# One weight tile of 128 partitions loaded in three pieces of 112, 15 - g and 1 + g partitions, in a decode attention kernel

## The chip, the cores and the metric

The kernel runs on one core of a Trainium2 chip. The metric is the device time of one execution in microseconds (us), taken as the median of several runs. Beside the runs stands one execution that the hardware profiler recorded; the views quoted in this text come from it.

## The reference

One token is decoded. Part A is attention of 32 heads with 65536 cached keys and values each, and an output projection; part B is a small gated feed-forward network; a sigmoid gate mixes the two.

```python
# x: 1x1x512, k_cache, v_cache: 1x32x65536x128 (bf16), wq: 512x4096, wo: 4096x512
q = (x @ wq) as 32 heads of 128
scores = einsum(q, k_cache) * 128 ** -0.5
p = softmax(scores)
o = einsum(p, v_cache)
a = o.reshape(1, 1, 4096) @ wo
b = (silu(x @ w_gate) * (x @ w_up)) @ w_down      # F = 1792
g = sigmoid((x * gate_w).sum())
out = g * a + (1 - g) * b
```

The caches hold 32 heads x 65536 x 128 x 2 bytes, twice: 1073.7 MB. All the weights together are 13.9 MB, of which `wo` is 4.2 MB.

## The kernel before

The caches are read in tiles of 4 MB: 128 partitions x 16384 elements of bf16. A head has G = 4 key tiles and 4 value tiles, so there are N = 128 of each. All of them go through `ring`, a pool of SLOTS = 5 buffers of that size, which `wq`, the gate and up weights and the down weights use as well at the start.

**Key tiles.** VectorE multiplies a key tile with the head's query (L220) and halves the 128 columns three times by adding (L224) down to 16; TensorE adds up the last 16 against an identity matrix (L234, `scores`). Once a head has all four tiles, its maximum, exponentials and sum are taken (`row_max`, `exponentials`, `total`).

**Value tiles.** TensorE multiplies the probabilities with the value tile, 32 matmuls of 128x512 per tile (L282, `values`). After a head's last value tile, `head_out` brings its output into one column of `oT` (L306 to L317), and `project` (L327) multiplies that column with the head's 128x512 part of `wo` and adds it into `a_ps`.

**Order.** The program fixes the order on every engine itself (`manual_schedule`). The list `steps` pairs a key tile with a value tile: values run G = 4 tiles behind keys at first and LAG = 8 later. In each step the loads are issued first, key tile, then (in one step of 16) the next group of `wo`, then the value tile. All loads are issued from SyncE's queue (SP), one after the other: a load that must wait for a free buffer holds up those behind it. The semaphores that tell of landings come from eight lanes used in turn, so a load also waits until the load eight places before it has landed.

**The last loads.** The value tiles of the last head come in halves, and the very last tile in four pieces of 64, 32, 16 and 16 columns (`CUTS`), so that the matmuls on the first pieces (`last_values`, L295) run while the last piece is on its way. Then come `weigh` (L317), `project` (L327), a cast (L398) and the store of the output (L399).

**wo.** `load_wo(g)` fetches group g of four heads (WG = 4) into a tile of 128 partitions x 4 x 512, out of `wo_pool` with two buffers. Partition p takes four rows of `wo`, one for each head, so each partition receives four runs of 1 KB. Group 0 is loaded at the start, behind the feed-forward weights; group g + 1 is loaded when value tile 16 g + 8 is due, and its first projection comes some 12 value tiles later. There are H / WG = 8 groups.

Of the kernel before, what the change touches and what calls it, by code (L numbers as in the profile page):

```python
# [11 lines left out]
P = 128  # L12
# [7 lines left out]

LAG = 8
SPREAD = 40

CUTS = (0, 64, 96, 112, 128)

# [2 lines left out]
def kernel(  # L28
# [14 lines left out]
    nc = tc.nc  # L43
# [99 lines left out]
    wo_tiles = {}  # L143

    def load_wo(g):
        wo_tiles[g] = wo_pool.tile([P, WG, D], bf16, name="wo_sb")
        rows = A_wo[g * WG * P : (g + 1) * WG * P, :]
        nc.sync.dma_start(out=wo_tiles[g], in_=rows.rearrange("(h p) n -> p h n", p=P))

    load_wo(0)  # L150

    def feed_forward_in():
# [185 lines left out]
    for n in range(N):  # L338
        due = n >= G and not (n >= SPREAD and n % 4 == 3 and n - v < LAG)
        steps.append((n, v if due else None))  # L340
# [6 lines left out]
    for n, v in steps:  # L347
        if n is not None and n > 1:
            load(K_tiles, A_k_cache, n, "K_t")
        if v is not None:  # L350
            if v % (WG * G) == 2 * G and v // (WG * G) + 1 < H // WG:
                load_wo(v // (WG * G) + 1)
            halves = (0, NB // 2, NB) if v >= N - G else (0, NB)
            load(V_tiles, A_v_cache, v, "V_t", CUTS if v == N - 1 else halves)
# [75 lines left out]
```

## Time and profile before

| | |
|---|---|
| Time, median of 3 runs | 2544.31 us (2544.15 to 2545.1) |
| The profiled execution's own time | 2544.7 us |
| Its span, first to last instruction | 2542.9 us |
| DMA: share of 16 engines' span on queue q1 | 99.6% |
| Moved | 1088.63 MB, mean 428 GB/s |
| VectorE busy | 2174.6 us (86%) |
| TensorE busy | 1721.1 us (68%) |
| ScalarE busy | 75.9 us (3%) |
| Mean granted TensorE clock | 0.752 |
| `wo` loads | 8 of 512 KB, median 36.6 us from issue to landing |

The span is what the profile covers; 1.8 us of the profiled execution's own time lie outside it. "Share of 16 engines" is the time that all packets of a queue took, divided by sixteen times the span: the core has 16 DMA engines, and a transfer is shared out among them. A transfer has landed when all of the engines that carried it have reported, and the trace keeps the time of each of these reports, without the number of the engine. Queue q1 carries the program's own transfers; q8 and q14 are marked as carrying instructions.

### The profile page before, as it was taken

To read this page: it belongs to the slowest core of one execution; us is meant where nothing else is said; L and a number is where in the kernel's file an instruction comes from. 1 tells how busy PE (TensorE), PEld (TensorE's weight loads), DVE (VectorE), ACT (ScalarE), POOL (GpSimd) and SP (SyncE) were. 2 spreads that over 40 slices of the span, in tenths; PEclk is the share of its full clock that TensorE was granted. 3 is DMA by queue.
4 is the path that set the end of the run, shared out by engine and by line. 5 is a ranking of instruction groups with operands and counts; after the bars stand their busy time and mean duration, and the time that the engine had idled before them with its cause. 6 is when DMAs were issued, how large, how long until landed. Compare 5 with 4: busy or idle time off the path is not lost.

```text
span 2542.9 us, 15396 instructions
## 1 busy us (share of the span) xinstructions
PE 1721.1 (68%) x6818; PEld 705.6 (28%) x6818; DVE 2174.6 (86%) x779; ACT 75.9 (3%) x206; POOL 0.7 (0%) x6
## 2 busy tenths in 40 slices
PE   3576766766677656667676676667666676677768
PEld 2232222222222222222232222222222222222223
DVE  6999888888888999998888888888888888888870
ACT  1000000000000000000000000000000000000000
POOL 0000000000000000000000000000000000000000
PEclk7677777777777677776777777777777777777779
DMA  9999999999999999999999999999999999999998
GB/s 408 427 432 430 432 430 432 431 429 431 431 432 430 429 432 431 431 432 431 429 431 431 432 429 430 432 430 431 429 432 432 430 432 428 433 431 431 432 431 348
DMA packets 42884, 1088.63 MB, mean 428 GB/s; under 512 B 4673, under 2 KB 8770, under 8 KB 9026
## 3 DMA queue, kind: packets, MB, share of 16 engines
q1 hardware_dynamic: 42818, 1087.66, 99.6%
q8 instruction: 53, 0.87, 0.1%
q14 instruction: 13, 0.11, 0.0%
HBM read 1087.64 MB, written 0.00 MB: 428 GB/s over the span
## 4 chain that ended last, share of the span: by engine, by line
DMA 68%; PE 21%; DVE 11%; issue 1%; ACT 0%; SPq 0%; DVEq 0%
DMA V_t<-in_A_v_cache_dram 63%; PE O_ps L282 19%; DVE K_t L220 6%; DVE K_t L224 5%; DMA K_t<-in_A_k_cache_dram 4%; PE S_ps L234 1%; DMA wq_t<-in_A_wq_dram 0%; PE qg_ps L120 0%; DVE m L246 0%; PE oh_ps L308 0%; PE a_ps L207 0%; ACT P_sb L259 0%; DVE top L255 0%; ACT O_sb L306 0%; PE a_ps L327 0%
## 5 line engine op out<-in xcount | busy, mean ns | idle before, releaser
L282 PE MATMUL O_ps<-V_t,P_sb 128*4 128x512 bf16 x4064 | 1139.3, 450 | 499.6 <-DMA V_t<-in_A_v_cache_dram 497.4
L220 DVE TENSOR_TENSOR K_t<-K_t,q_bc 128x16384 bf16<-128x16384 bf16 (+1 forms) x159 | 1117.2, 7026 | 275.3 <-DMA K_t<-in_A_k_cache_dram 256.0
L224 DVE TENSOR_TENSOR K_t<-K_t 128x2048 bf16<-128x2048 bf16 (+3 forms) x477 | 1030.6, 2161 | 14.2
L282 PEld LDWEIGHTS <-P_sb 128*4 128x4 bf16 x4064 | 389.4, 96 | 1229.9 <-issue 883.3
L234 PE MATMUL S_ps<-K_t,ident_b 128*128 128x128 bf16 x2048 | 464.6, 392 | 123.8 <-DVE K_t L224 123.8
L234 PEld LDWEIGHTS <-ident_b 128*128 128x128 bf16 x2048 | 225.6, 114 | 346.9 <-issue 153.1
L308 PE MATMUL oh_ps<-ident_f,O_sb 4*128 4x1 f32 x256 | 57.2, 340 | 74.0 <-ACT O_sb L306 74.0
L250 PE MATMUL mT_ps<-diag,ones_f 128*128 128x128 f32 x64 | 23.6, 468 | 80.8 <-ACT diag L248 80.8
L308 PEld LDWEIGHTS oh_ps<-ident_f,O_sb 4*128 4x128 f32 x256 | 54.5, 310 | 83.1 <-ACT O_sb L306 78.8
L248 ACT ACTIVATE diag<-ident_f,m 128x128 f32<-128x128 f32 x32 | 12.8, 401 | 2108.3 <-DVE m L246 2108.3
L398 DVE CAST out_sb<-a_ps 1x512 bf16<-1x512 f32 x1 | 0.7, 677 | 52.4 <-PE a_ps L327 52.4
L250 PEld LDWEIGHTS mT_ps<-diag,ones_f 128*128 128x128 f32 x64 | 14.8, 288 | 96.6 <-ACT diag L248 96.6
L246 DVE TENSOR_REDUCE m<-S_ps 128x1 f32<-128x512 f32 x32 | 21.9, 684 | 7.4 <-PE S_ps L234 7.4
L259 ACT ACTIVATE P_sb<-S_ps,bias 128x512 bf16<-128x512 f32 x32 | 22.0, 687 | 1.0
L306 ACT ACTIVATE O_sb<-O_ps 4x512 f32<-4x512 f32 x32 | 18.3, 573 | 123.1 <-PE O_ps L282 123.1
L120 PE MATMUL qg_ps<-wq_t,X_bc 128*128 128x512 bf16 x32 | 8.5, 431 | 14.1 <-DMA wq_t<-in_A_wq_dram 14.1
L185 PE MATMUL b_ps<-wd_t,hT 128*1 128x512 bf16 x14 | 5.7, 597 | 15.7 <-DVE hT L178 15.7
L273 DVE RECIPROCAL recip<-tot_ps 128x1 f32<-128x1 f32 x32 | 5.1, 160 | 12.2 <-PE tot_ps L268 12.2
L327 PE MATMUL a_ps<-wo_sb,oT 128*1 128x512 bf16 x32 | 13.5, 423 | 0.4 <-ACT oT L317 0.4
L268 PEld LDWEIGHTS tot_ps<-rowsum,ones_f 128*128 128x128 f32 x64 | 9.5, 188 | 14.0 <-issue 14.0
L268 PE MATMUL tot_ps<-rowsum,ones_f 128*128 128x1 f32 x64 | 12.2, 260 | 0.0
L317 ACT ACTIVATE oT<-oh_ps,rg 128x1 bf16<-128x1 f32 x32 | 8.4, 264 | 81.2 <-PE oh_ps L308 75.0
(39 smaller groups left out, 69.1 us busy)
## 6 DMA issues: line engine op xcount, KB each, us to landing
K_t<-in_A_k_cache_dram SPq DMA_DIRECT2D x128, 4096.0 KB, 35.3
V_t<-in_A_v_cache_dram SPq DMA_DIRECT2D x124, 4096.0 KB, 29.7
V_t<-in_A_v_cache_dram SPq DMA_DIRECT2D x7, 2048.0 KB, 31.8
wq_t<-in_A_wq_dram SPq DMA_DIRECT2D x1, 4096.0 KB, 12.4
wo_sb<-in_A_wo_dram SPq DMA_DIRECT2D x8, 512.0 KB, 36.6
gu_t<-in_B_w_gate_dram SPq DMA_DIRECT2D x1, 1792.0 KB, 34.7
gu_t<-in_B_w_up_dram SPq DMA_DIRECT2D x1, 1792.0 KB, 38.4
wd_t<-in_B_w_down_dram SPq DMA_DIRECT2D x1, 1792.0 KB, 42.2
```

What stands on the lines that cost most here:

```text
L220: yield nc.vector.tensor_tensor(out=K, in0=K, in1=q_rep, op=ALU.mult)
L224: yield nc.vector.tensor_tensor(out=K[:, :, 0:half], in0=K[:, :, 0:half], in1=K[:, :, half : 2 * half], op=ALU.add,)
L234: nc.tensor.matmul(S_tiles[h][:, g * NB : (g + 1) * NB], lhsT=ident_b, rhs=K_tiles[n][:, :, c], start=(c == 0), stop=(c == WIDTH - 1),)
L246: nc.vector.tensor_reduce(out=m, in_=S_tiles[h], axis=AXIS.X, op=ALU.max)
L248: nc.scalar.activation(out=diag, in_=ident_f, func=ACT.Copy, scale=m)
L250: nc.tensor.matmul(mT_ps, lhsT=ones_f, rhs=diag, start=True, stop=True)
L259: nc.scalar.activation(out=P_tiles[h], in_=S_tiles[h], func=ACT.Exp, bias=bias, scale=scale, accum_out=rowsum[:, h : h + 1],)
L268: nc.tensor.matmul(tot_ps, lhsT=ones_f, rhs=rowsum[:, h : h + 1], start=True, stop=True)
L282: nc.tensor.matmul(O_tiles[h], lhsT=P_tiles[h][:, g * NB + j : g * NB + j + 4], rhs=V_tiles[n][:, j : j + 4, :], start=(g == 0 and j == 0) ...
L306: nc.scalar.activation(out=O_sb, in_=O_tiles.pop(h), func=ACT.Copy)
L308: nc.tensor.matmul(oh_ps, lhsT=O_sb[:, c * Dh : (c + 1) * Dh], rhs=ident_f[0:4, c : c + 1], start=(alone and c == 0), stop=(alone and c == 3),
L327: nc.tensor.matmul(a_ps, lhsT=oT[:, h : h + 1], rhs=wo_tiles[h // WG][:, h % WG, :], start=False, stop=(h == H - 1),)
```

## The change

`load_wo` no longer issues one transfer for the 128 partitions of a group but three: partitions 0 to 111, the next 15 - g, and the last 1 + g. The bytes, the tile, its place in the order and everything that reads it stay as they are. Over the eight groups the second piece has 15, 14, ... 8 partitions and the third 1, 2, ... 8.

```diff
+WO_BULK = 7
...
     def load_wo(g):
         wo_tiles[g] = wo_pool.tile([P, WG, D], bf16, name="wo_sb")
         rows = A_wo[g * WG * P : (g + 1) * WG * P, :]
-        nc.sync.dma_start(out=wo_tiles[g], in_=rows.rearrange("(h p) n -> p h n", p=P))
+        rows = rows.rearrange("(h p) n -> p h n", p=P)
+        for a, b in ((0, 16 * WO_BULK), (16 * WO_BULK, P - 1 - g), (P - 1 - g, P)):
+            nc.sync.dma_start(out=wo_tiles[g][a:b], in_=rows[a:b])
```

The program's instructions on the compute engines are the same and in the same order; SP issues 16 more transfers. As each transfer takes the next of the eight semaphore lanes, the lanes that later loads wait on move as well. Behind each later group this asks for no landing that the ring of five buffers does not ask for anyway. At the start it does: the third piece of group 0 waits for the landing of `wq`, and the third key tile, which waited for `wq` and the queries made from it, now waits for the landing of the first key tile as well.

## The prediction

> **What bounds the kernel now.** I read the page's DMA rows first, then stretches of time, then the landing records, then SP's timeline.
>
> ```profile
> span 2542.9 us, 15396 instructions
> ...
> GB/s 408 427 432 430 432 430 432 431 429 431 431 432 430 429 432 431 431 432 431 429 431 431 432 429 430 432 430 431 429 432 432 430 432 428 433 431 431 432 431 348
> DMA packets 42884, 1088.63 MB, mean 428 GB/s; under 512 B 4673, under 2 KB 8770, under 8 KB 9026
> ...
> q1 hardware_dynamic: 42818, 1087.66, 99.6%
> q8 instruction: 53, 0.87, 0.1%
> q14 instruction: 13, 0.11, 0.0%
> ```
>
> The rate stays at 428 to 433 GB/s from the third slice to the last but one, and the packets fill 99.6% of sixteen engines' time. VectorE at 86% and TensorE at 68% have room. So the end is set by the DMA engines, and by the one with the most to do. The chain of waits runs through the value loads and the matmuls that free their buffers; with the engines full, that is the way the queue is refilled, not a second limit. The next view has us from:to, length, busy time of PE, PEld, DVE, ACT and POOL, the granted clock, the DMA share and GB/s.
>
> ```profile
> 1200.00:1210.00 10.00, 5.21 (x17) 1.77 (x17) 9.93 (x3) 0.00 (x0) 0.00 (x0) 0.59 1.01 427
> 2520.00:2526.00 6.00, 6.00 (x30) 2.38 (x28) 0.00 (x0) 0.00 (x0) 0.00 (x0) 1.00 0.98 411
> 2526.00:2528.00 2.00, 1.58 (x8) 0.51 (x6) 0.00 (x0) 0.00 (x0) 0.00 (x0) 1.00 0.70 293
> 2530.00:2532.00 2.00, 2.00 (x11) 0.69 (x9) 0.00 (x0) 0.00 (x0) 0.00 (x0) 1.00 0.54 227
> 2534.00:2536.00 2.00, 2.00 (x59) 1.98 (x55) 0.00 (x0) 0.00 (x0) 0.00 (x0) 1.00 0.47 186
> 2537.00:2538.00 1.00, 0.84 (x27) 0.69 (x24) 0.00 (x0) 0.00 (x0) 0.00 (x0) 0.50 0.06 25
> 2538.00:2540.00 2.00, 1.13 (x17) 0.58 (x17) 0.00 (x0) 0.27 (x1) 0.00 (x0) 0.50 0.00 0
> ```
>
> Here the engines run out one by one. A share of 0.54 is some nine of sixteen; 0.06 is a single one, alone on the last microsecond. The trace's landing records say how far apart they are. Each transfer has sixteen; those of the last one lie 0, 0.2, 0.3, 0.6, 0.7, 1.3, 3.3, 6.7, 9.2, 9.5, 10.2, 10.3, 10.6, 10.8, 11.0 and 12.4 us behind the first, 6.1 on average. So five engines are early, three in between, eight late, and one is last by 1.4 us. The last one's distance grows in steps of about 1.55 us: 3.1 us at 125 us, 6.2 at 878, 9.2 at 1639, 10.85 at 2019, 12.4 at 2477. The packets of q8 explain it: 53 of 16 KB, each some 1.05 us long, with lengths that recur after every eighth. Eight engines take turns to fetch them, and one such packet and the slower one beside it cost its engine about 1.55 us. At 115 us the queue ran dry for a moment (V tiles issued at 113.80 us); after that no engine but the early ones at the very end has an idle stretch. Whatever the last engine carries is paid for, microsecond for microsecond: from its last landing at 2538.5 us the tail of matmul, scale, projection, cast and store takes 4.4 us, whatever came before.
>
> **The change, part by part.**
>
> *Bytes moved between engines.* The eight `wo` transfers land 1.45 to 1.49 us after the transfer before them on the first engine (1.48 for group 0). That is eight partitions on each engine, 32 packets of 1 KB, thus 1.47 / 8 = 0.184 us a partition. How will the new pieces be shared out? The page's counts show both ends: 276 loads with 16 reports each make 4416, and 4673 - 256 (the 8-byte packets of `xT` and `gwT`) - 4416 leaves one report for the output store. A load of 128 partitions is spread evenly over 16; a transfer with one row went to one engine. 112 is 7 each; 15 - g and 1 + g have no even sixteenths. Bounds: an engine left out by both pieces in all groups loses 8 x 0.184 = 1.47 us; one that got all 16 partitions of the two pieces each time would gain 8 x (16 - 1) x 0.184 = 22.1 us over now. The nearest row is the even spread of the 276 loads, all of 128 partitions, so I take one partition per engine, with both pieces starting at the same end of the sixteen. Then the engine nearest that end carries 8 more partitions in all (+1.47 us), the next 7 more, the eighth 1 more; the ninth 1 less, the sixteenth 8 less (-1.47 us). Nothing else in the change can bring anything.
>
> [...]
>
> *16 more transfers.* The last tile's pieces are queued one behind another like these: the landings of its four pieces on the first engine are 2.49, 1.26 and 1.27 us apart for 1 MB, 512 KB and 512 KB, which is 8 packets of 0.312 or 0.157 us and 0.01 of rest. So a transfer within a full queue costs an engine about 0.01 us: 16 x 0.01 = 0.2 us at most. An exposed transfer would be 1.8 us (`xT`, `gwT`, issue to landing); the full queue is the cover, and without it 16 x 1.8 = 29 us would be due.
>
> *SP.* Each issue takes 0.43 us:
>
> ```profile
> 510.02 0.33 SPq L111 DMA_DIRECT2D V_t<-in_A_v_cache_dram  x1
> 513.58 0.33 SPq L111 DMA_DIRECT2D K_t<-in_A_k_cache_dram  x1
> 513.96 0.43 SPq L148 DMA_DIRECT2D wo_sb<-in_A_wo_dram  x1
> 529.98 0.33 SPq L111 DMA_DIRECT2D V_t<-in_A_v_cache_dram  x1
> ```
>
> Two more (0.9 us) fit into the 15.6 us in which SP waits for the next value tile's buffer. Even a late issue would be covered: a tile lands 30 to 35 us after its issue and takes 9.7 us of the engines, so about two more are queued ahead of it. Cost 0; uncovered, 8 x 0.9 = 7 us.
>
> *Waits at the start.* The third piece of group 0 waits for `wq` (14.05 us in SP's rows), and the third key tile, issued at 22.59 us, now waits for the first one, whose sixteen landings lie between 23.2 and 23.8 us. It goes up to 1.2 us later, while the queue holds work until group 0 lands at 47.3 us. The fourth and fifth key tiles (44.3 and 51.0 us) wait for landings that were over by 38. Cost 0. Until 115 us VectorE sets the pace (9.78 of 10 us busy at 100 to 110), so group 0's shift may be lost when the queue runs dry: seven groups then count, 1.29 instead of 1.47 us.
>
> *Readers of `wo`.* A projection waits for three landings instead of one, some 12 value tiles after the issue, over 200 us for a landing of 37. Cost 0.
>
> **The sum.** Last engine among the relieved eight: 0.2 to 1.5 us less; among the loaded eight: 0.2 to 1.5 more. The second-last is 1.4 us ahead, so it hardly cuts the gain. The records do not number the engines; the order in which they report at the start puts early and late ones side by side and decides nothing. I take the relieved side, as a choice, and the mean of one to eight partitions: 4.5 x 0.184 = 0.8 us. The profiled execution goes from 2542.9 + 1.8 = 2544.7 to 2543.9; it was 0.4 over the median, so the median goes from 2544.3 to 2543.5. 0.2% (5 us) is about what a measurement of this kernel can tell from no change.
>
> **The rivals.**
> - *Forecast, the last engine is relieved:* 2542.8 to 2544.1. For: the shift only reaches the end by the last engine, and half of the engines are relieved. 0.50.
> - *The last engine is loaded:* the eight fetching engines are those that get the second partition. 2544.5 to 2545.8, slower by less than 0.1%. 0.25.
> - *It cancels:* the last engine is near the middle, or the 0.2 us of completions eat the shift. 2544.1 to 2544.5. 0.18.
> - *An odd piece is not spread:* one engine takes all partitions of the small pieces, as one took the store's row. It gets up to 22.1 us more. If it is an early one it has 12.4 us to spare and ends 9.7 us late: 2554; if it is the last, 2566. It decides as soon as one engine gets over 67 partitions more (12.4 / 0.184). Against it: every load with many partitions is spread. 0.05, slower.
> - *More than the shift:* all of the imbalance gone is 12.4 - 6.1 = 6.3 us, 2538, just past 0.2%. Eight partitions can't do that. 0.02, faster.
>
> Runs scatter over 0.95 us, half of it on either side: low 2544.31 - 1.47 - 0.5 = 2542.3, high 2544.31 + 1.47 + 0.5 = 2546.3. That holds the first three cases, 0.93 less a little at the edges. Faster 0.02, same 0.93, slower 0.05.
>
> **What the profile after would show.** q1 with the same bytes, share at 99.6%, and the last landing at 2537.0 to 2538.3 instead of 2538.5 us: right. One engine alone for more than 1.4 us at the end: the loaded side. 1 KB packets piled on one engine, and a DMA share near 0.06 for ten microseconds: not spread. If slices in the middle fall below 428 GB/s, the small transfers cost what I put at 0.01 us. A landing spread that is the same with another time would prove the shift irrelevant.

## The result, and the profile after

The changed kernel takes 2569.13 us (median of 5 runs, 2566.54 to 2573.14), against 2544.15 us before (2543.03 to 2545.1) in the same comparison: a ratio of 1.01, interval 1.0089 to 1.011. It is 25 us slower, where 0.8 us less was forecast. The profiled execution took 2569.56 us, with a span of 2567.8 us.

The page's rows after, as shown of before:

```profile
span 2567.8 us, 15408 instructions
...
GB/s 404 428 431 412 431 431 432 432 408 432 431 432 431 409 431 432 431 430 425 412 431 432 430 415 420 431 430 432 405 426 431 431 432 399 433 431 430 432 432 350
DMA packets 43015, 1088.63 MB, mean 424 GB/s; under 512 B 4804, under 2 KB 8901, under 8 KB 9157
...
q1 hardware_dynamic: 42949, 1087.66, 99.7%
q8 instruction: 53, 0.87, 0.1%
q14 instruction: 13, 0.11, 0.0%
```

The bytes are the same and the engines are as busy as before (99.7%), but the same work took longer. The loss is not spread out: the rate stands at 428 to 433 GB/s in most slices and dips to 399 to 420 in a few, where a group of `wo` is loaded. What the engines do there is seen in stretches of 2 us around the third group, after first and then before (the last two columns are the DMA share and GB/s):

```profile
547.00:549.00 2.00, 2.00 (x11) 0.82 (x10) 1.97 (x2) 0.00 (x0) 0.00 (x0) 1.00 1.12 323
549.00:551.00 2.00, 2.00 (x11) 0.65 (x10) 0.42 (x1) 0.00 (x0) 0.00 (x0) 1.00 1.02 224
551.00:553.00 2.00, 2.00 (x11) 1.09 (x11) 0.00 (x0) 0.00 (x0) 0.00 (x0) 1.00 1.04 248
553.00:555.00 2.00, 1.60 (x8) 0.59 (x6) 1.01 (x1) 0.00 (x0) 0.00 (x0) 1.00 1.00 270
555.00:557.00 2.00, 0.00 (x0) 0.00 (x0) 2.00 (x1) 0.00 (x0) 0.00 (x0) 0.82 1.02 426
```

```profile
544.00:546.00 2.00, 2.00 (x11) 0.79 (x10) 1.97 (x2) 0.00 (x0) 0.00 (x0) 1.00 1.00 399
546.00:548.00 2.00, 2.00 (x11) 0.68 (x8) 0.78 (x1) 0.00 (x0) 0.00 (x0) 1.00 0.98 380
548.00:550.00 2.00, 2.00 (x10) 1.03 (x10) 0.49 (x1) 0.00 (x0) 0.00 (x0) 1.00 1.11 462
```

Before, the rate hardly falls while a group passes. After, it halves for about 8 us, and no engine is idle: the packets themselves are slow. In the trace the 1 KB packets of `wo` take 78 ns at the median instead of 46, and packets of 32 KB, which belong to the cache tiles beside them and were not touched by the change, take more than 1.4 us 593 times instead of 93, at worst 2.6 us (2.2 before) instead of the usual 1.215. Added up and divided by sixteen, the 1 KB packets cost 20.0 - 12.5 = 7.5 us more, and the excess of the 32 KB packets over 1.215 us rose from 7.8 to 26.3, by 18.5 us. The sum, 26 us, is the whole loss, and over two thirds of it fall on neighbours.

The other places that the prediction named:

```profile
512.71 0.33 SPq L113 DMA_DIRECT2D V_t<-in_A_v_cache_dram  x1
516.27 0.33 SPq L113 DMA_DIRECT2D K_t<-in_A_k_cache_dram  x1
516.64 1.25 SPq L152 DMA_DIRECT2D wo_sb<-in_A_wo_dram  x3
530.97 0.35 SPq L113 DMA_DIRECT2D V_t<-in_A_v_cache_dram  x1
```

SP issues the three transfers within 1.25 us and still waits 13 us for the next value tile's buffer. At the end of the span the engines run out one by one as before, 25 us later:

```profile
2552.00:2560.00 8.00, 5.46 (x81) 2.92 (x79) 0.00 (x0) 0.59 (x1) 0.00 (x0) 0.99 0.56 232
2560.00:2563.00 3.00, 3.00 (x56) 2.97 (x54) 0.00 (x0) 0.00 (x0) 0.00 (x0) 0.50 0.12 45
2563.00:2565.00 2.00, 1.45 (x28) 0.78 (x25) 0.07 (x1) 0.26 (x1) 0.00 (x0) 0.50 0.00 0
```

The last landing is at 2563.3 instead of 2538.5 us, and the sixteen landings of the last transfer are spread over 12.2 us instead of 12.4: the imbalance between the engines, at which the change could aim, is as it was.

### The profile page after: what moved, and what is told of

It is laid out like the page before. It is cut to its first block, busy times and chain, and to the rows that moved or that the text cites. A ratio compares the mean times of both kernels' runs of the same rounds, so it can differ in the third digit from the quotient of the medians.

```text
span 2567.8 us, 15408 instructions
## 1 busy us (share of the span) xinstructions
PE 1721.2 (67%) x6818; PEld 706.9 (28%) x6818; DVE 2174.6 (85%) x779; ACT 75.9 (3%) x206; POOL 0.7 (0%) x6
## 3 DMA queue, kind: packets, MB, share of 16 engines
q1 hardware_dynamic: 42949, 1087.66, 99.7%
## 4 chain that ended last, share of the span: by engine, by line
DMA 69%; PE 20%; DVE 9%; SPq 1%; issue 1%; ACT 0%; DVEq 0%
DMA V_t<-in_A_v_cache_dram 62%; PE O_ps L286 19%; DMA K_t<-in_A_k_cache_dram 7%; DVE K_t L224 5%; DVE K_t L228 4%; PE S_ps L238 1%; SPq L152 1%; DVE m L250 0%; PE oh_ps L312 0%; PE a_ps L211 0%; ACT P_sb L263 0%; DVE top L259 0%; SPq L113 0%; ACT O_sb L310 0%; PE a_ps L331 0%
## 5 line engine op out<-in xcount | busy, mean ns | idle before, releaser
L277 DVE RECIPROCAL recip<-tot_ps 128x1 f32<-128x1 f32 x32 | 5.1, 160 | 12.4 <-PE tot_ps L272 12.4
L272 PE MATMUL tot_ps<-rowsum,ones_f 128*128 128x1 f32 x64 | 12.2, 260 | 0.0
```

Source lines behind the costliest of these rows:

```text
L272: nc.tensor.matmul(tot_ps, lhsT=ones_f, rhs=rowsum[:, h : h + 1], start=True, stop=True)
```

## The experiments

The first question was what is slow: the number of transfers, the uneven pieces, or the place that the pieces have. Of `load_wo` only the transfers are shown. In all of them `rows` is the rearranged slice, as in the change. Each comparison has its own runs of the kernel before, so its time differs a little from one to the next.

**Three whole transfers.** As many as in the changed kernel, each of 128 partitions.

```diff
+        for a, b in ((0, 2), (2, 3), (3, 4)):
+            nc.sync.dma_start(out=wo_tiles[g][:, a:b], in_=rows[:, a:b])
```

> Each group of wo comes in three transfers, but of all 128 partitions: heads 0 and 1, head 2, head 3 (256, 128 and 128 KB). So there are as many transfers as in the changed kernel (24), and every engine carries in each what it carries in any 128-partition load. Theory P (placement: a DMA engine that writes other partitions than those it writes in a 128-partition load gets in the way of the engines that write there): 2544 us, within 2 of before. Theory N (number: each extra transfer costs some 1.6 us, 25 / 16): 2569. Theory U (uneven: the pieces that not all sixteen engines carry are at fault): 2544. In P and U the 1 KB packets take 46 ns at the median as before, in N they may take longer.

Measured: 2543.43 us against 2543.75, ratio 1.0 (0.9991 to 1.0009); 1 KB packets at 46 ns.

```profile
GB/s 408 428 434 429 430 431 432 431 428 431 431 431 431 430 430 431 432 431 431 429 432 430 431 429 431 432 430 432 429 431 432 432 430 429 432 431 430 433 430 354
```

There are no dips: 16 more transfers cost nothing that can be measured. The number is out.

**112 and 16 partitions.** Both pieces are even shares for sixteen engines.

```diff
+        for a, b in ((0, 112), (112, P)):
+            nc.sync.dma_start(out=wo_tiles[g][a:b], in_=rows[a:b])
```

> Two transfers per group, of 112 and 16 partitions, seven and one for each engine: no piece is uneven, but both are shifted against the places of a 128-partition load. P: most of the 25 us, 2560 to 2569, and 1 KB packets near 78 ns at the median as in the changed kernel. N: 8 extra transfers, 12.5 us, 2556.5. U: 2544.

Measured: 2568.2 us against 2543.75, ratio 1.01 (1.0085 to 1.0115), 1 KB packets at 78 ns, and the same half rate around the third group:

```profile
547.00:549.00 2.00, 2.00 (x11) 0.77 (x9) 1.11 (x1) 0.00 (x0) 0.00 (x0) 1.00 1.01 229
549.00:551.00 2.00, 2.00 (x10) 0.86 (x9) 0.00 (x0) 0.00 (x0) 0.00 (x0) 1.00 1.09 239
551.00:553.00 2.00, 2.00 (x11) 1.03 (x9) 0.00 (x0) 0.00 (x0) 0.00 (x0) 1.00 1.07 269
```

This has all of the change's cost without an uneven piece. What the uneven pieces do to the balance of the engines is lost in the scatter of these runs.

**64 and 64 partitions.**

```diff
+        for a, b in ((0, 64), (64, P)):
+            nc.sync.dma_start(out=wo_tiles[g][a:b], in_=rows[a:b])
```

> Two transfers per group, of partitions 0 to 63 and 64 to 127, four partitions for each engine. P: 2556 to 2575, since four partitions per engine are again not the places of a 128-partition load. [...] N: 2556.5. U: 2544.

Measured: 2574.93 us against 2543.75, ratio 1.0124 (1.0109 to 1.0139). That is 31 us, more than for 112 and 16, and at the upper end of what placement (theory P) led one to expect. Neither the number (12.5 us) nor unevenness (none) gives it.

**The whole transfer, and the uneven pieces beside it.** The pieces go into a spare tile that nothing reads.

```diff
+        nc.sync.dma_start(out=wo_tiles[g], in_=rows)
+        spare = spare_pool.tile([P, WG, D], bf16, name="spare")
+        for a, b in ((112, P - 1 - g), (P - 1 - g, P)):
+            nc.sync.dma_start(out=spare[a:b], in_=rows[a:b])
```

> Each group of wo comes in one transfer of 128 partitions as before, and the two small pieces of the changed kernel (15 - g and 1 + g partitions) come again, into a spare tile that nothing reads. So the uneven pieces and the number of transfers are those of the changed kernel, with the transfer of 112 made whole. Bytes: 0.5 MB more, 1.2 us. P: 16 instead of 128 shifted partitions a group, an eighth of 25, so 2546 to 2550. N: 2570. U: 2565 to 2571.

Measured: 2549.8 us against 2543.75, ratio 1.0023 (1.0014 to 1.0033). The uneven pieces are worth 6 us, of which an estimated 1.2 us are the extra bytes that only this run moves. If the parts add up, the other 19 to 20 us of the change come from the transfer of 112.

So the partitions that a transfer covers matter. The second question was whether that is a matter of the shape, of the reading side, or of the partitions that are written. Three runs keep the whole transfer and add 256 KB more per group to the spare tile, differently placed.

**Extra 256 KB, all partitions.**

```diff
+        nc.sync.dma_start(out=wo_tiles[g], in_=rows)
+        spare = spare_pool.tile([P, WG, D], bf16, name="spare")
+        nc.sync.dma_start(out=spare[:, 0:2], in_=rows[:, 0:2])
```

> Each group of wo comes in one transfer as before; heads 0 and 1 of it (256 KB, 128 partitions) come once more into a spare tile that nothing reads. This prices the bytes alone: half of 1.47 us a group, 5.9 us in all, 2549.6 us, in every theory. 1 KB packets at 46 ns.

Measured: 2549.55 us against 2543.96, ratio 1.0022 (1.0013 to 1.0031). The bytes alone cost 5.6 us; the 1 KB packets took 48 ns at the median, near the expected 46.

**Extra 256 KB to partitions 32 to 95.**

```diff
-        nc.sync.dma_start(out=spare[:, 0:2], in_=rows[:, 0:2])
+        nc.sync.dma_start(out=spare[32:96], in_=rows[32:96])
```

> As the run with the half columns, but the extra 256 KB are partitions 32 to 95 of the group, written to partitions 32 to 95 of the spare tile, four for each engine. [...] Theory S (shape: every transfer of fewer than 128 partitions disturbs, wherever it goes): half of the 31 us that 64 + 64 partitions cost, and the bytes, 2565 us.

Measured: 2549.37 us against 2543.96, ratio 1.0022 (1.0012 to 1.0032). Beside the 5.6 us of the bytes this placement costs nothing that can be measured; the 1 KB packets took 48 ns here too.

**Extra 256 KB, the same rows, to partitions 0 to 63.**

```diff
-        nc.sync.dma_start(out=spare[32:96], in_=rows[32:96])
+        nc.sync.dma_start(out=spare[0:64], in_=rows[32:96])
```

> The same 256 KB, read from the same rows as in the run before, with the same share for each engine, but written to partitions 0 to 63 of the spare tile. Only the destination differs. [...] Theory S: 2565 us, the same as the run before. Theory R (the reading side is at fault, the order of the rows in HBM): the same as the run before, whatever that is.

Measured: 2567.42 us against 2543.96, ratio 1.0094 (1.0079 to 1.0109). That is 18 us more than the run before. Their rates in the 40 slices, partitions 32 to 95 first, 0 to 63 second:

```profile
GB/s 409 429 431 428 432 431 432 428 431 429 434 429 432 428 431 433 429 434 430 429 430 430 433 428 431 430 432 430 430 430 431 433 431 429 431 430 432 430 434 355
```

```profile
GB/s 401 432 432 413 433 429 431 431 415 431 432 432 429 414 430 433 430 432 428 416 431 431 433 421 422 432 432 431 415 426 432 431 431 410 432 432 430 431 431 352
```

The dips come and go with the destination's partitions, and with nothing else: bytes, source rows, shape, share of each engine and number of transfers are the same. For these 256 KB that settles the side and refutes the theories of the shape and of the reading. The median of the 1 KB packets hides part of it, since two thirds of them are those of the whole transfer: it is 53 ns, while the upper quarter around each group begins at 55 to 91 ns (51 to 52 in the run before). That the destination's partitions matter is shown; why 0 to 63 cost 18 us and 32 to 95 nothing is not: no trace tells which engine wrote what.

**wo in 32 to 95, 0 to 31, 96 to 127.**

```diff
+        for a, b in ((32, 96), (0, 32), (96, P)):
+            nc.sync.dma_start(out=wo_tiles[g][a:b], in_=rows[a:b])
```

> Each group of wo in three transfers of partitions 32 to 95, 0 to 31 and 96 to 127; bytes as before. [...] Theory S: 2569 to 2580, no better than 64 + 64.

Measured: 2557.73 us against 2543.96, ratio 1.0056 (1.0041 to 1.0071). 13.8 us, somewhat under half of the 31 us of 64 and 64: with one more transfer it costs less. The piece of 32 to 95 goes where the extra 256 KB cost no more than their bytes; if that holds here too, the 13.8 us come from the other two pieces, half of the partitions.

**Value tiles in 64 and 64.** The last question was whether small packets are needed for this. One value tile in sixteen was split, with packets of 32 KB, and `wo` left whole.

```diff
+PARTS = ((0, 64), (64, 128))
...
+        if name == "V_t" and n % 16 == 8:
+            for a, b in PARTS:
+                nc.sync.dma_start(out=view[a:b], in_=src[a:b])
+            dst[n] = view
+            return
```

> wo comes in one transfer per group as before. Instead, one value tile in sixteen (8 tiles of 4 MB, packets of 32 KB) comes in two transfers of partitions 0 to 63 and 64 to 127. [...] Theory T (only the 1 KB packets of wo are sensitive): 2544.

Measured: 2704.12 us against 2543.88, ratio 1.0641 (1.0607 to 1.0674). That is 160 us, or 20 us for each of eight tiles on average. Small packets aren't needed for the effect. Its size is twice what a half rate within the split tiles alone would give: a whole tile of 4.2 MB takes 9.7 us at 431 GB/s, so eight would lose an estimated 8 x 9.7 = 78 us. (Here the rows that are read change together with the partitions that are written, so this run does not tell the two sides apart.) The rate in slices of 3.5 us, from 480 to 620 us, around the second of the tiles:

```profile
GB/s 417 431 424 449 431 412 431 431 449 421 431 440 431 431 421 417 449 421 440 431 440 403 274 221 215 215 197 227 215 290 431 440 435 421 421 421 440 440 421 440
```

The rate is about half for 28 us, in which about 6.5 MB move: the 4.2 MB of the tile and some 2.3 MB of its neighbours. At 431 GB/s the same bytes would take 15 us, so this tile loses 13. The estimate of 9.7 us a tile slows the tile alone.

Not all of the 160 us are of this kind. The 1 KB packets of the third to the eighth group of `wo` begin 11.7, 24.6, 38.7, 53.4, 69.0 and 95.9 us later than before, so each of the first five split tiles costs 12 to 16 us and the sixth 27. And at the end of the trace one engine works alone for some 20 us:

```profile
2669.00:2674.00 5.00, 5.00 (x25) 1.97 (x24) 0.00 (x0) 0.00 (x0) 0.00 (x0) 1.00 0.07 29
2674.00:2689.00 15.00, 12.36 (x158) 6.99 (x156) 0.00 (x0) 0.59 (x1) 0.00 (x0) 0.98 0.06 27
```

Of the sixteen landings of the last transfer, fifteen lie between 2663.2 and 2668.6 us and the last one at 2689.8. So the split value tiles also cost the engines unequally; in the trace of 64 and 64 partitions of `wo` the last landing was 5.2 us behind the next, instead of 1.4.

**Value tiles in 32 to 95, 0 to 31, 96 to 127.**

```diff
-PARTS = ((0, 64), (64, 128))
+PARTS = ((32, 96), (0, 32), (96, 128))
```

> The same eight value tiles in three transfers of partitions 32 to 95, 0 to 31 and 96 to 127. [...] Theory T: 2544.

Measured: 2645.52 us against 2543.88, ratio 1.0386 (1.0354 to 1.0417). 102 us: again less than with two halves, by about a third. Here too one engine is left at the end, 16.9 us behind the next.

None of these gives a version faster than before, so none was built on them. The best a full balance of the engines could bring is 12.4 - 6.1 = 6.3 us, and the uneven pieces cost some 5 us by themselves, 6 with the extra bytes.

## Why the prediction was wrong, point by point

**What bounds the kernel** was right: the DMA engines, at 99.6% before and 99.7% after, and whatever slows them comes through to the end almost unchanged (26 us of packet time, 25 us of time).

**The step that failed** is the one on bytes moved between engines. It priced a partition at 0.184 us wherever it goes, asked only which engine carries it, and closed with "Nothing else in the change can bring anything." In the trace of before every load has 128 partitions; 46 ns for a 1 KB packet and 1.215 us for one of 32 KB were prices for that, and I took them for prices of the packet. Where the prediction had nothing more, the runs showed 26 us of packet time: 7.5 in the packets of `wo` themselves and 18.5 in their neighbours. With 112 and 16 partitions the cost was 24 us, with the same bytes in three whole transfers 0.

**How the pieces are shared out** was taken rightly. Before, 4417 packets of 4 bytes report landings; after, there are 4548. The 131 more are 15 + 14 + ... + 8 = 92 for the second pieces and 2 + 3 + ... + 8 = 35 for the third, and 4 are left for the third piece of group 0: one partition of four runs went to four engines. So the rival "not spread", whose price of 10 to 22 us came nearest, had the wrong mechanism; no engine was piled on.

**16 more transfers** at 0.01 us each was right (three whole transfers, 2543.43 us). The 29 us (16 x 1.8) that it named for transfers without the cover of a full queue look close to the 25 that were measured, but by luck: the same number of whole transfers cost nothing. For the same reason its sign "if slices in the middle fall below 428 GB/s" misled. They did fall, to 399, but not because of the number of transfers.

**SP, the waits at the start and the readers of `wo`** at 0: nothing contradicts it. SP's three issues took 1.25 us of the 14 us until its next load. At the start the third key tile was issued at 24.34 instead of 22.59 us, 1.75 us later and not at most 1.2, but the fourth and the fifth were issued at 44.32 and 50.97 us, as before.

**The sign of the shift** could not be isolated, because the uneven pieces also cost time of their own (6 us beside the whole transfer, extra bytes included). The run with the whole transfer and the pieces beside it gives a hint: for g = 4 to 6 the engine that lands last in the whole transfer does not appear among the 11, 10 and 9 landings of the second piece, so it is one of those that the change relieves; for g = 7 the order of the landings leaves it open. The spread at the end was 12.2 us in the changed kernel against 12.4, but this decides little: in the traces of kernels without uneven pieces that cost no more than their bytes it lies between 11.1 and 12.4 us, which is as much as the shift was to bring. So the side that the prediction chose is neither confirmed nor refuted.

**What stays open:** why some destinations cost time, and why the neighbours lose so much. That some 2.3 MB of the tiles next to a split value tile were slowed too was measured and not explained. With 112 and 16 partitions the 1 KB packets were as slow as with 64 and 64 (78 and 80 ns at the median). The loss also grows along the run: in the changed kernel the excess of the 32 KB packets, divided by sixteen, rises from 2.3 us around the second group to 4.7 around the eighth (0.6 and 1.2 before), while the engines drift apart (the 1 KB packets of the second group begin within 6.1 us of each other, those of the eighth within 16.0; 4.5 and 12.3 before); whether the one causes the other was not tested. For the transfer of 112 itself, reading and writing were not separated: that its destination is at fault is concluded from the 64 partitions. A 128-partition load that reached its places in another order was not tried.

## What to carry to other kernels

Where a profile shows the DMA engines full, as here, load tiles over all 128 partitions and cut them along the free dimension if they must be cut: three such pieces cost nothing, 112 + 16 partitions cost 24 us on 4 MB of weights. If a cut along partitions is needed, the destination decided in the one pair of runs that tells: the middle 64 (32 to 95) cost no more than their bytes and the first 64 cost 18 us more, from the same source. And a duration read from a trace holds for the conditions under which it was measured; ask what all the rows of that trace have in common that the change gives up.

## What was not expected of the hardware

In the changed kernel the pieces of `wo` slowed transfers that have nothing to do with them: over two thirds of the loss fell on untouched 32 KB packets (18.5 of 26 us), which took up to 2.6 instead of 1.215 us. Value tiles in 64 and 64 partitions also left one engine some 20 us behind the others. The runs of the changed kernel scatter more, 2566.5 to 2573.1 us against 2543.0 to 2545.1. And the sixteen engines are uneven by 12.4 us at the end of the unchanged kernel, for the most part, it seems, since the 53 instruction packets of 16 KB go to eight of them in turn (their lengths recur after every eighth), at about 1.55 us each: the lag of the last engine rises from 6.2 to 7.7, 9.2, 10.85 and 12.4 us, a step every eight such packets.
